# Head 1's K rows shifted by GpSimd instead of copied twice by ScalarE, in a chunk-selected attention with an MLP

## The chip, the core and the metric

The kernel runs on one core of a Trainium2 chip. The core has TensorE (PE, matrix multiplications into PSUM), VectorE (DVE), ScalarE (ACT), GpSimd (POOL), SyncE (SP, here an issuer of DMAs), 16 DMA engines, and the on-chip memories SBUF (128 partitions) and PSUM. GpSimd works on SBUF alone in this kernel. The metric is the device time of one execution, in microseconds.

## The reference

Four batches, eight heads, 768 positions, 64 dimensions a head. For each query, the keys are taken in chunks of 32; an upper bound of the score of each chunk is built from the chunk's elementwise minimum and maximum, the six best chunks that causality allows are kept, and softmax attention runs over these. The result goes through an MLP with 2048 hidden units and an ELU.

```python
k_min, k_max = np.min(k_chunks, axis=3), np.max(k_chunks, axis=3)
ub = np.sum(np.maximum(q * k_min, q * k_max), axis=-1)          # per query and chunk
ub = np.where(causal, ub, -1e9)
top_chunks = np.argsort(ub, axis=-1)[..., -6:]
scores = np.where(sel & causal_by_position, q @ k.T / 8, -1e9)
x = softmax(scores) @ v                                          # 3072 x 512 over all heads
h = x @ w_in
out = np.where(h > 0, h, np.exp(np.minimum(h, 0)) - 1) @ w_out
```

## The kernel before, in words

**Units of work.** Two heads make a pair (16 pairs, four a batch, numbered 0 to 15), two pairs a quad. The 768 positions are worked on in two halves of 384. Batch 0 (pairs 0 to 3, the tuple SPLIT) is prepared half by half in `first_prep`, since it stands at the start; the other batches are prepared pair by pair in `pair_prep`. Selection is `quad_sel`, attention `pair_attend`, the MLP of a batch and half `mlp`.

**Preparing batch 0.** K and Q of a pair and half are loaded row by row (L755), 192 KB each; V follows (L760). The constant EARLY says of how many pairs Q is issued from ScalarE's queue; the rest is issued by SyncE. TensorE turns each tile (L780, six f32 transposes): both heads' 64 dimensions then lie below each other on 128 partitions of PSUM. From the turned K, ScalarE makes two copies into the pair's bf16 tile `lhs` (L797): head 0's 64 partitions to rows 0 to 63 of the first plane, and head 1's partitions 64 to 127 to rows 0 to 63 of the second. VectorE takes the chunks' minima and maxima from the same PSUM (L806) and their difference (L813). From the turned Q, ScalarE makes an f32 copy (L830) and a relu (L837), both for the bounds, and GpSimd casts the copy to bf16 for both heads (L853). GpSimd casts V (L844).

**Selection inside the scores.** Rows 64 to 87 of `lhs` hold a one-hot pattern of the chunks times a large negative number (`econ`, written once per tile by VectorE at L584, from a table that ScalarE makes at L558), and rows 64 to 87 of the query tile `rhs` hold ones where a chunk is not selected. So one matmul over 88 rows gives scores and mask together. For the first 192 positions, where all allowed chunks are selected, these query rows are zero (memsets at L572).

**Selection.** TensorE makes the bounds (L890) from Q, its relu and the chunk tables; VectorE transposes them (L906), takes the eight largest (L918), compares (L923) and transposes back (L929); GpSimd copies the result into `rhs` (L940).

**Attention.** Scores (L995; in the first half of batch 0 TensorE adds the causal mask too, L1001), exp by ScalarE (L1023), the causal mask of diagonal blocks elsewhere by GpSimd (L1042), probabilities times V with a column of ones (L1055), reciprocal and scaling by VectorE (L1068, L1071), and a transpose into `xT`, by TensorE and ScalarE (L1104, L1107) or by VectorE and a DMA.

**MLP.** Up-projection in 16 blocks of 128 hidden units (L1133), exp (L1142), and on some blocks a relu on ScalarE (L1147); VectorE finishes the ELU into `gT` (L1150, or L1183 and L1188); down-projection (L1204), copy (L1213), store (L1218). The weights come in four quarters each, issued by GpSimd (L636, L640).

**Preparing the other batches.** K and Q are loaded in 128-byte pieces (L682), transposed in blocks by VectorE (L694, L712), reduced (L698), cast by GpSimd (L853); the relu for the bounds is ScalarE's (L715, 128x576 f32); V has its own load and cast (L726, L730).

**Order.** Each engine's order is written out as a list of operation numbers (`QUEUE`, lists for DVE, POOL, ACT, SP and PE), found beforehand. `Plan.order` merges the five lists into one program; each engine then executes its own list strictly in order and waits where data or a buffer is not there. Buffers are pools whose sizes stand in `caps`; who gets which buffer follows from that merged order.

Of the kernel before, what the change touches and what calls it, by code (L numbers as in the profile page):

```python
# [12 lines left out]
AF = mybir.ActivationFunctionType  # L13
# [5 lines left out]
S = 768  # L19
# [40 lines left out]
VMERGE = 10  # L60
LAST = ((0, 256), (256, 128), (384, 128))

EARLY = (4, 0)
QUEUE = {
    "DVE": [
# [21 lines left out]
    ],  # L87
    "POOL": [
# [11 lines left out]
    ],  # L100
    "ACT": [
# [20 lines left out]
    ],  # L122
# [8 lines left out]
    ],  # L131
# [295 lines left out]
def kernel(  # L427
# [64 lines left out]
    def place(h, slot):  # L492
# [5 lines left out]
        elif c in kept:  # L498
            tiles[h] = kept[c][slot]
        elif c in shapes:  # L500
            shape, dt = ([P, 8, HALF], F32) if h in STAGED.values() else shapes[c]
            tiles[h] = work.tile(shape, dt, name=f"{c}_{h[1]}", tag=f"{c}{slot}")
# [784 lines left out]
```

## Time and profile before

| | us |
|---|---|
| three runs | 268.28, 263.69, 267.38 |
| their median | 267.38 |
| the profiled execution | 263.55 |
| its span, from the first instruction to the last | 261.8 |
| TensorE busy | 256.1 (98%) |
| VectorE busy | 207.5 (79%) |
| ScalarE busy | 193.1 (74%) |
| GpSimd busy | 121.1 (46%) |

The page of the profile gives busy times of a whole execution. Other views of the same trace cut it into stretches, group instructions by source line, list who waited for whom, or follow the chain of work that ended last. A duration in such a row is that of one instruction unless it says xN; matmuls overlap, so their mean durations add up to more than the time they take. A DMA row gives the time from issue to landing.

### The profile page before, as it was taken

The page shows a single profiled execution, that of the slowest core. Times are in us where ns is not written, and L with a number is a line of the kernel's source. Part 1 is how long each engine was busy: PE and PEld are TensorE (multiplying, and loading weights), DVE is VectorE, ACT ScalarE, POOL GpSimd, SP SyncE. Part 2 cuts the span into 40 slices and gives each one's busy share as a digit, 9 for nine tenths or more (in the row PEclk, how much of TensorE's full clock was granted, in tenths as well). Part 3 has the DMA queues.
Part 4 walks back from the last instruction along what each step waited for, and adds up shares of the span by engine and source line. Part 5 has one row for each costly group of instructions (what it writes and reads, how often), then busy time and mean ns, then how long its engine had stood idle before and what let it go on. Part 6 is the DMA issues. An engine that isn't in the chain of part 4 may idle for free.

```text
span 261.8 us, 6681 instructions
## 1 busy us (share of the span) xinstructions
PE 256.1 (98%) x2416; PEld 158.4 (60%) x2416; DVE 207.5 (79%) x545; ACT 193.1 (74%) x364; POOL 121.1 (46%) x216
## 2 busy tenths in 40 slices
PE   8999989999999999999999999999999999999995
PEld 7888556655556655657555456656565755455544
DVE  4999998999999999998899886987465897335530
ACT  4999989927897899898997567988879554043332
POOL 2688668746737868866641319866302000000000
PEclk9999999999999999999999999999999999999999
DMA  7999999999999979349958393323033012220123
GB/s 218 318 200 170 179 179 133 188 203 134 166 150 213 199 137 134 80 80 210 171 99 179 56 254 82 87 73 95 8 84 106 18 30 66 89 83 12 68 92 112
DMA packets 127010, 33.74 MB, mean 129 GB/s; under 512 B 112897, under 2 KB 124033, under 8 KB 126977
## 3 DMA queue, kind: packets, MB, share of 16 engines
q1 hardware_dynamic: 121664, 28.33, 53.5%
q0 software_dynamic: 4224, 4.19, 10.4%
q10 hardware_dynamic: 1088, 0.79, 1.0%
q8 instruction: 19, 0.31, 0.5%
q14 instruction: 15, 0.11, 0.2%
HBM read 29.23 MB, written 8.26 MB: 143 GB/s over the span
## 4 chain that ended last, share of the span: by engine, by line
PE 83%; DMA 8%; SPq 5%; ACT 1%; ACTq 1%; issue 1%; POOL 0%; POOLq 0%
PE psM L1204 24%; PE psH L1133 22%; PE psS L995 12%; PE psS L1133 8%; PE psO L1055 7%; PE psMT L1204 7%; DMA w_in_sb<-in_moe_w_in_dram 4%; SPq L682 3%; PE psS L890 3%; DMA gT<-in_q_dram 2%; SPq L760 2%; DMA out_dram<-osb 1%; DMA gT<-in_v_dram 1%; ACTq L755 1%; PE psT L1104 1%
## 5 line engine op out<-in xcount | busy, mean ns | idle before, releaser
L1023 ACT ACTIVATE pt<-psS 128x768 bf16<-128x768 f32 (+1 forms) x120 | 89.9, 787 | 10.9 <-PE psS L995 6.2
L1133 PE MATMUL psH<-xT,w_in_sb 128*128 128x384 bf16 x384 | 75.1, 325 | 0.8 <-DMA w_in_sb<-in_moe_w_in_dram 0.8
L1204 PE MATMUL psM<-w_out_sb,gT 128*128 128x512 bf16 x288 | 72.2, 379 | 0.0
L1133 PEld LDWEIGHTS <-w_in_sb 128*128 128x128 bf16 x512 | 47.4, 97 | 33.9 <-issue 1.3
L1204 PEld LDWEIGHTS <-gT 128*128 128x128 bf16 x416 | 37.9, 97 | 34.7 <-issue 0.6
L1142 ACT ACTIVATE f<-psH 128x384 f32<-128x384 f32 x96 | 48.0, 513 | 12.9 <-PE psH L1133 12.4
L995 PE MATMUL psS<-rhs,lhs 88*128 88x384 bf16 (+4 forms) x304 | 53.6, 283 | 0.2
L1042 POOL TENSOR_SCALAR_AFFINE_SELECT pt<-pt 128x256 bf16<-128x256 bf16 (+1 forms) x56 | 28.9, 523 | 47.2 <-ACT pt L1023 46.4
L1055 PEld LDWEIGHTS <-pt 128*128 128x128 bf16 x672 | 31.0, 98 | 10.2 <-ACT pt L1023 0.5
L995 PEld LDWEIGHTS <-lhs 88*128 88x128 bf16 x304 | 26.9, 98 | 13.6 <-ACT pt L1023 1.0
L1055 PE MATMUL psO<-vext,pt 128*128 128x65 bf16 x672 | 34.7, 194 | 0.0
L1150 DVE SCALAR_TENSOR_TENSOR gT<-f,psH 128x384 bf16<-128x384 f32 x48 | 25.5, 541 | 10.7 <-ACT psH L1147 10.6
L853 POOL CAST rhs<-f 64x768 bf16<-64x768 f32 (+1 forms) x40 | 27.6, 692 | 10.7 <-ACT f L830 7.4
L1183 DVE SCALAR_TENSOR_TENSOR t<-f,psH 128x384 bf16<-128x384 f32 x48 | 25.7, 539 | 6.6 <-ACT f L1142 6.3
L940 POOL COPY rhs<-selt 24x576 bf16<-24x576 bf16 (+2 forms) x40 | 22.6, 564 | 18.1 <-DVE selt L929 16.1
L1142 ACT ACTIVATE f<-psS 128x768 f32<-128x768 f32 x16 | 13.0, 814 | 22.9 <-PE psS L1133 22.9
L1188 DVE SCALAR_TENSOR_TENSOR gT<-psH,t 128x384 bf16<-128x384 f32 x48 | 26.1, 549 | 0.8
L1147 ACT ACTIVATE psH<-psH 128x384 f32<-128x384 f32 x48 | 24.6, 520 | 0.0
L1133 PE MATMUL psS<-xT,w_in_sb 128*128 128x384 bf16 x128 | 22.9, 326 | 0.0
L1204 PE MATMUL psMT<-w_out_sb,gT 128*128 128x512 bf16 (+2 forms) x128 | 22.1, 326 | 0.0
L1172 DVE TENSOR_SCALAR t<-f 128x768 bf16<-128x768 f32 x16 | 8.9, 556 | 15.7 <-ACT f L1142 15.7
L853 POOL CAST lhs<-f 64x768 bf16<-64x768 f32 x24 | 19.6, 820 | 0.7
(59 smaller groups left out, 273.4 us busy)
## 6 DMA issues: line engine op xcount, KB each, us to landing
out_dram<-osb SPq DMA_DIRECT2D x23, 256.0 KB, 2.2
f<-in_k_dram SPq DMA_DIRECT2D x48, 96.0 KB, 3.8
f<-in_q_dram SPq DMA_DIRECT2D x48, 96.0 KB, 3.7
f<-in_v_dram SPq DMA_DIRECT2D x10, 384.0 KB, 4.4
w_in_sb<-in_moe_w_in_dram POOLq DMA_DIRECT2D x4, 512.0 KB, 9.1
w_out_sb<-in_moe_w_out_dram POOLq DMA_DIRECT2D x4, 512.0 KB, 7.4
xd<-on SPq DMA_DIRECT2D x80, 24.0 KB, 1.6
xT<-xd SPq DMA_DIRECT2D x20, 96.0 KB, 2.2
```

Of the source, the lines that this page charges most:

```text
L853: nc.gpsimd.tensor_copy(out=o, in_=i)
L995: nc.tensor.matmul(p_s[:, hd, pc:pc + w], lhsT=tiles[pt_["kb"]][0:deep(hd), hd, 128 * kb:128 * kb + 128], rhs=tiles[pt_["qb"]][0:deep(hd), ...
L1023: lambda bs=bs, pt=pt, wtot=wtot, lo=lo, at=at: nc.scalar.activation(out=tiles[pt][:, :, lo:lo + wtot], in_=tiles[bs[0]][:, :, at:at + wto ...
L1042: nc.gpsimd.affine_select(out=a, in_=a, compare_op=AOT.is_ge, fill=0.0, base=0, pattern=pat, channel_multiplier=-1)
L1055: nc.tensor.matmul(po[:, hd, qi, :], lhsT=tiles[pt][:, hd, off:off + 128], rhs=tiles[pt_["vx"]][:, 6 * hd + kb, :], start=(kb == 0), stop= ...
L1133: nc.tensor.matmul(o, lhsT=w_in_sb[:, kk, f0:f0 + 128], rhs=rhs, start=(kk == 0), stop=(kk == NKK - 1))
L1142: lambda e=e, view=view: nc.scalar.activation(out=halves(e)[:, 0:step], in_=view(), func=AF.Exp),
L1147: lambda view=view: nc.scalar.activation(out=view(), in_=view(), func=AF.Relu),
L1150: lambda e=e, view=view, fc=fc, gt=gt: nc.vector.scalar_tensor_tensor(out=tiles[gt][:, fc:fc + step, :], in0=halves(e)[:, 0:step], scalar= ...
L1183: lambda e=e, t=t, view=view: nc.vector.scalar_tensor_tensor(out=tiles[t][:, 0:step], in0=halves(e)[:, 0:step], scalar=1.0, in1=view(), op ...
L1188: lambda t=t, view=view, fc=fc, gt=gt: nc.vector.scalar_tensor_tensor(out=tiles[gt][:, fc:fc + step, :], in0=view(), scalar=0.0, in1=tiles ...
L1204: nc.tensor.matmul(pm, lhsT=tiles[gt][:, fc, 128 * tt:128 * tt + 128], rhs=w_out_sb[:, fc, x0:x1], start=(fc == 0), stop=(fc == NFC - 1))
```

## The change

Names and lines of the diff are those of the kernel before.

- In batch 0, both halves (KSHIFT), ScalarE copies all 128 partitions of the turned K at once into the first plane of `lhs`. Head 1's rows, which now lie on partitions 64 to 127 of that plane, are copied by GpSimd to rows 0 to 63 of the second plane. After that VectorE writes the one-hot rows of the first plane (`mark`), once per pair and half, since the copy has overwritten them. Scores that use the rows wait for the mark, except those of the first 192 positions.
- VectorE no longer writes the first plane's one-hot rows of pairs 0 to 3 at the start.
- The relus of pairs 4 and 5 (RELUP2) are made by GpSimd.
- 14 load buffers `f` instead of 13; four relu buffers `qa` instead of three; a probability tile has 384 columns a head instead of 512.
- In two probability tiles the order of the two key blocks is swapped, so that the two diagonal blocks adjoin.
- Q of pairs 2 and 3 is issued by SyncE (EARLY 2 instead of 4).
- All five lists are new.
- Other new parameters (RELUDVE, RELUPOOL, UBTWO, NXT, NON, NPT) are empty or have the old value.

```diff
+RELUPOOL = ()
+KSHIFT = (0, 1)
+RELUP2 = (4, 5)
+NF = 14
+NQA = 4
...
-EARLY = (4, 0)
+EARLY = (2, 0)
 QUEUE = {
...
-            "f": 13, "qa": 3, "kb": 5, "qb": 5, "vx": 5, "kx": 2, "km": 4,
+            "f": NF, "qa": NQA, "kb": 5, "qb": 5, "vx": 5, "kx": 2, "km": 4,
...
-        "pt": ([P, 2, 512], BF16), "t": ([P, 2, HALF], BF16),
+        "pt": ([P, 2, HALF], BF16), "t": ([P, 2, HALF], BF16),
...
                 r = slice(0, 64) if HIGH and hd else slice(64, 96)
+                if hd == 0 and i < 4 and KSHIFT:
...
+                    continue
                 eng.tensor_copy(out=kept["kb"][i][r, hd, :], in_=econ[r])
...
-        add("ACT", act(S - SEL0) + 0.036, pr + 0.1,
-            lambda: nc.scalar.activation(out=tiles[qa], in_=tiles[qt][:, SEL0:S], func=AF.Relu),
-            reads=[qt], writes=[qa], alloc=[qa])
+        if u in RELUP2:
+            add("POOL", pool(S - SEL0), pr + 0.1,
+                lambda: nc.gpsimd.tensor_scalar_max(tiles[qa], tiles[qt][:, SEL0:S], 0.0),
+                reads=[qt], writes=[qa], alloc=[qa], tag="qrelu2")
...
+    def mark(u, hf, pr):
+        kb = PAIR[u]["kb"]
+        a, b = HALF * hf, HALF * hf + HALF
+        add("DVE", 0.2, pr, lambda: nc.vector.tensor_copy(out=tiles[kb][64:96, 0, a:b], in_=econ[64:96, a:b]),
+            reads=["econ", (kb, hf, 1)], writes=[(kb, hf, "m")], port=True, tag="mark")
...
-        for hd in () if KTWO else range(2):
+        if hf in KSHIFT:
+            add("ACT", act(HALF), pr,
+                lambda: nc.scalar.activation(out=tiles[kb][:, 0, a:b], in_=ps(bk, None, None)[:, :], func=AF.Copy),
+                reads=[bk[0]], writes=[(kb, hf, 0), (kb, hf, "m"), (bk[0], "turn")], alloc=[] if hf else [kb], tag="kcopy0")
+            add("POOL", pool(HALF), pr + 0.02,
+                lambda: nc.gpsimd.tensor_copy(out=tiles[kb][0:64, 1, a:b], in_=tiles[kb][64:128, 0, a:b]),
+                reads=[(kb, hf, 0), (kb, hf, "m")], writes=[(kb, hf, 1)], tag="kcopy1")
+            if hf:
+                mark(u, hf, pr + 0.3)
+        for hd in () if KTWO or hf in KSHIFT else range(2):
...
-        0: [[(0, 0, 384, 0)], [(1, 128, 256, 0), (2, 256, 128, 256)]],
+        0: [[(0, 0, 384, 0)], [(2, 256, 128, 0), (1, 128, 256, 128)]],
...
-            [(3, 384, 384, 0)], [(4, 512, 256, 0), (5, 640, 128, 256)]],
+            [(3, 384, 384, 0)], [(5, 640, 128, 0), (4, 512, 256, 128)]],
...
+                marked = [(pt_["kb"], i, "m") for i in range(hf + 1) if i in KSHIFT] if u in SPLIT else []
+                if marked and hf == 0 and pi == 1:
+                    mark(u, 0, pr - 0.3)
...
-                    + [(pt_["qb"], hf, hd) for hd in range(2)]
+                    + [(pt_["qb"], hf, hd) for hd in range(2)] + marked
...
-                                a = tiles[pt].rearrange("p h (a b) -> p (h a) b", b=256)[:, :, 0:128]
+                                a = tiles[pt][:, :, 0:256]
```

More of the change, by code (lines that the diff above doesn't have):

```diff
@@ L60 @@
 VMERGE = 10
+RELUDVE = ()
+RELUPOOL = ()
+KSHIFT = (0, 1)
+RELUP2 = (4, 5)
+UBTWO = ()
+NF = 14
+NQA = 4
+NXT = 8
+NON = 4
+NPT = 10
 LAST = ((0, 256), (256, 128), (384, 128))
-EARLY = (4, 0)
+EARLY = (2, 0)
 QUEUE = {
     "DVE": [
[21 rows of a table removed]
[22 rows of a table added]
     ],
     "POOL": [
[11 rows of a table removed]
[12 rows of a table added]
     ],
     "ACT": [
[20 rows of a table removed]
[20 rows of a table added]
     ],
     "SP": [
[7 rows of a table removed]
[7 rows of a table added]
     ],
     "PE": [
[32 rows of a table removed]
[31 rows of a table added]
     ],
@@ L438 @@
     caps = {"S2": 2, "ps": 4, "H": 3, "O": 2, "T": 2, "M": 2, "MT": 2,
-            "f": 13, "qa": 3, "kb": 5, "qb": 5, "vx": 5, "kx": 2, "km": 4,
-            "ubt": 1, "thr": 1, "selv": 1, "selt": 2, "pt": 10, "t": 3, "gT": 3,
-            "osb": 3, "on": 4, "rc": 3, "xT": 8}
+            "f": NF, "qa": NQA, "kb": 5, "qb": 5, "vx": 5, "kx": 2, "km": 4,
+            "ubt": 1, "thr": 1, "selv": 1, "selt": 2, "pt": NPT, "t": 3, "gT": 3,
+            "osb": 3, "on": NON, "rc": 3, "xT": NXT}
     plan = Plan(caps)
@@ L499, in place @@
             tiles[h] = kept[c][slot]
+            assert not KSHIFT or c != "kb" or slot < 4 or h not in [PAIR[u]["kb"] for u in SPLIT]
         elif c in shapes:
@@ L583, in f @@
                 r = slice(0, 64) if HIGH and hd else slice(64, 96)
+                if hd == 0 and i < 4 and KSHIFT:
+                    for x in range(2):
+                        if x not in KSHIFT:
+                            eng.tensor_copy(out=kept["kb"][i][r, 0, HALF * x:HALF * x + HALF], in_=econ[r, HALF * x:HALF * x + HALF])
+                    continue
                 eng.tensor_copy(out=kept["kb"][i][r, hd, :], in_=econ[r])
@@ L618 @@
             continue
-        add("DVE", 0.6, (-5.0, -4.0, 0.9, 0.95, 2.0)[i], c_rows(i), reads=["econ"] + (["elow"] if HIGH else []), writes=[("rows", i)], port=True)
+        add("DVE", 0.6 - (0.3, 0.13)[2 - len(KSHIFT)] if i < 4 and KSHIFT else 0.6, (-5.0, -4.0, 0.9, 0.95, 2.0)[i], c_rows(i), reads=["econ"] + (["elow"] if HIGH else []), writes=[("rows", i)], port=True)
     v3 = v.rearrange("b h (n p) d -> p (b h n) d", p=P)
@@ L669 @@
     SELT = {}
+    BU = {}
     XT = {}
@@ L713, in pair_prep @@
             reads=[qd], writes=[qt], alloc=[qt], free=[qd])
-        add("ACT", act(S - SEL0) + 0.036, pr + 0.1,
-            lambda: nc.scalar.activation(out=tiles[qa], in_=tiles[qt][:, SEL0:S], func=AF.Relu),
-            reads=[qt], writes=[qa], alloc=[qa])
+        if u in RELUP2:
+            add("POOL", pool(S - SEL0), pr + 0.1,
+                lambda: nc.gpsimd.tensor_scalar_max(tiles[qa], tiles[qt][:, SEL0:S], 0.0),
+                reads=[qt], writes=[qa], alloc=[qa], tag="qrelu2")
+        else:
+            add("ACT", act(S - SEL0) + 0.036, pr + 0.1,
+                lambda: nc.scalar.activation(out=tiles[qa], in_=tiles[qt][:, SEL0:S], func=AF.Relu),
+                reads=[qt], writes=[qa], alloc=[qa])
         for hd in range(2):
@@ L830, in first_prep @@
             lambda: nc.scalar.activation(out=tiles[qt][:, qo[0]:qo[0] + QW], in_=ps(bq, None, None)[:, 0:QW], func=AF.Copy),
-            reads=[bq[0]], writes=[qt], alloc=[qt], tag="qcopy")
+            reads=[bq[0]], writes=[qt], alloc=[qt], free=bq if (u, hf) in RELUPOOL else [], tag="qcopy")
         lo = max(a, SEL0)
@@ L835, in first_prep @@
         PAIR[u]["ao", hf] = la
-        add("ACT", act(l1 - l0), pr + 0.05,
-            lambda: nc.scalar.activation(out=tiles[qa][:, la:la + l1 - l0], in_=ps(bq, None, None)[:, l0:l1],
-                                         func=AF.Relu),
-            reads=[bq[0]], writes=[qa], alloc=[qa], free=bq, tag="qrelu")
+        if (u, hf) in RELUPOOL:
+            add("POOL", pool(l1 - l0), pr + 0.05,
+                lambda: nc.gpsimd.tensor_scalar_max(tiles[qa][:, la:la + l1 - l0],
+                                                    tiles[qt][:, qo[0] + l0:qo[0] + l1], 0.0),
+                reads=[qt], writes=[qa], alloc=[qa], tag="qrelu")
+        elif (u, hf) in RELUDVE:
+            add("DVE", dve(l1 - l0), pr + 0.05,
+                lambda: nc.vector.tensor_scalar_max(tiles[qa][:, la:la + l1 - l0], ps(bq, None, None)[:, l0:l1], 0.0),
+                reads=[bq[0]], writes=[qa], alloc=[qa], free=bq, tag="qrelu")
+        else:
+            add("ACT", act(l1 - l0), pr + 0.05,
+                lambda: nc.scalar.activation(out=tiles[qa][:, la:la + l1 - l0], in_=ps(bq, None, None)[:, l0:l1],
+                                             func=AF.Relu),
+                reads=[bq[0]], writes=[qa], alloc=[qa], free=bq, tag="qrelu")
         for hd in range(2):
@@ L873, in quad_sel, with ub @@
             bu = new("S2")
-            def ub(bu=bu, c0=c0, n=n, nh=nh):
+            both = whole and g // 2 in UBTWO
+            if both and g % 2:
+                bu = BU[g]
+            def ub(bu=bu, c0=c0, n=n, nh=nh, pairs=pairs):
                 pu = tiles[bu[0]]
@@ L894, in quad_sel @@
             fr = []
-            for u in pairs:
+            for u in pairs if not both else range(4 * (g // 2), 4 * (g // 2) + 4):
                 rd += [PAIR[u]["qt", hf], PAIR[u]["qa", hf]] + [(PAIR[u]["km"], i, x) for i in range(2) for x in hs]
@@ L899, in quad_sel, with ubs @@
                     fr += [PAIR[u]["km"]]
-            add("PE", 0.00167 * n + 0.27, pr, ub, ins=64, reads=rd, writes=[bu[0]], alloc=bu, free=fr)
+            if both and g % 2 == 0:
+                b2 = BU[g + 1] = new("S2")
+                p2 = (pairs[0] + 2, pairs[1] + 2)
+                def ubs(ub=ub, b2=b2, p2=p2):
+                    ub()
+                    ub(bu=b2, pairs=p2)
+                add("PE", 2 * 0.00167 * n + 0.27, pr, ubs, ins=128, reads=rd, writes=[bu[0], b2[0]], alloc=bu + b2, free=fr)
+            elif not both:
+                add("PE", 0.00167 * n + 0.27, pr, ub, ins=64, reads=rd, writes=[bu[0]], alloc=bu, free=fr)
             ut, = new("ubt")
@@ L1027, in pair_attend @@
                         free=bs if si == len(shares) - 1 else [])
-                    done = {0: tiles_by_half[0], 1: tiles_by_half[1]}[hf][ti]
+                    done = ([[(0, 0, 384, 0)], [(1, 128, 256, 0), (2, 256, 128, 256)]] if pieces is FIRST else tiles_by_half[hf])[ti]
                     if pi < len(pieces) - 1 and pieces is FIRST and ti:
@@ L1033, in pair_attend @@
                     diag = [pc for (kb, c0, w, pc) in done if c0 == 128 * kb]
+                    assert onpe or diag in ([], [0], [0, 128])
                     if diag and not onpe:
@@ L1138, in mlp @@
                     free=[XT[4 * b + kk] for kk in range(NKK)] if hf and fc == NFC - step else [])
-                both = fc in BOTH[b]
+                both = fc in BOTH.get((b, hf), BOTH[b])
                 e, = new("f")
```

183 rows, old and new, of the table QUEUE are left out of this document.

## The prediction

> **What bounds the kernel now.** I read the busy shares first, then TensorE's busy time in stretches, then the waits and the chain of the stretch that is not full.
>
> ```profile
> PE 256.1 (98%) x2416; PEld 158.4 (60%) x2416; DVE 207.5 (79%) x545; ACT 193.1 (74%) x364; POOL 121.1 (46%) x216
> 0.00:4.00 4.00, 2.94 (x28) 2.90 (x28) 1.44 (x8) 1.11 (x1) 1.85 (x16) 1.00 0.47 140
> 4.00:24.00 20.00, 19.85 (x292) 17.44 (x289) 18.21 (x77) 18.87 (x47) 12.96 (x28) 1.00 1.08 243
> 24.00:40.00 16.00, 14.41 (x165) 8.91 (x164) 14.89 (x42) 15.26 (x30) 11.20 (x23) 1.00 1.13 181
> 40.00:100.00 60.00, 60.00 (x605) 36.01 (x604) 58.75 (x139) 49.95 (x92) 41.43 (x66) 1.00 1.07 170
> 100.00:160.00 60.00, 60.00 (x536) 34.97 (x535) 54.11 (x154) 48.56 (x95) 31.69 (x50) 1.00 0.71 141
> ```
>
> The columns after the length are TensorE, its weight loads, VectorE (DVE), ScalarE (ACT), GpSimd (POOL), then the granted clock and the DMA share. From 40 us on TensorE is full (60.00 of 60.00), and the number of its instructions is the same in both kernels. So time can be won only where TensorE is idle: 0.15 us between 4 and 24, 1.59 between 24 and 40, 1.74 in all, beside the start. The ends of matmuls are modelled, so each gap may hide a little more; I allow as much again, 3.6 us, as the most that this change can give. In the same two stretches ACT (18.87 of 20, 15.26 of 16) and DVE (18.21, 14.89) are nearly full and POOL is not (12.96, 11.20). The change takes work from ACT and gives it to POOL and DVE in just these stretches.
>
> What TensorE waits for between 4 and 40 us, and the chain up to the longest of these waits:
>
> ```profile
> PEld L1104 <- DVE on L1071: 1.3, 3, 0.6
> PEld L995 <- ACT pt L1023: 1.0, 3, 0.5
> PE psH L1133 <- DMA w_in_sb<-in_moe_w_in_dram: 0.8, 1, 0.8
> PEld psS L890 <- ACT lhs L797: 0.2, 1, 0.2
> ...
> 2.37 5.91 DMA gT<-in_q_dram
> 25.71 0.64 POOL w_in_sb L636
> 26.35 10.04 DMA w_in_sb<-in_moe_w_in_dram
> 36.44 0.84 PE psH L1133 x4
> ```
>
> The longest single gap (0.8) is the third quarter of w_in: issued by POOL at 26.35, landed at 36.39, needed by the sixth up-projection in TensorE's list (fc 8). Waits on ACT come to 1.2 (scores waiting for an exp to free their PSUM, and one for a K copy); waits on DVE's normalized outputs stand ahead of the transposes that feed the first MLP.
>
> **The change part by part.** Rows for the prices:
>
> ```profile
> L797 ACT ACTIVATE lhs<-psH 64x384 bf16<-64x384 f32 x16 | 7.8, 485 | 0.8 <-PE psH L780 0.7
> L830 ACT ACTIVATE f<-psMT 128x384 f32<-128x384 f32 x8 | 3.9, 493 | 0.2 <-PE psMT L780 0.2
> L715 ACT ACTIVATE qa<-f 128x576 f32<-128x576 f32 x12 | 8.3, 692 | 0.8 <-DVE f L712 0.8
> L844 POOL CAST vext<-gT 128x384 bf16<-128x384 f32 x8 | 3.9, 503 | 0.4
> L730 POOL CAST vext<-f 128x768 bf16<-128x768 f32 x12 | 9.9, 824 | 4.0 <-DMA f<-in_v_dram 3.7
> 16.89 0.34 POOL L940 COPY rhs<-selt 24x192 bf16<-24x192 bf16 x1
> 10.01 0.62 DVE L584 COPY lhs<-econ 32x768 bf16<-32x768 bf16 x2
> 8.16 0.76 DVE L584 COPY lhs<-econ 32x768 bf16<-32x768 bf16 x2
> ```
>
> *K copies.* Of 16 ACT copies of 0.485, eight remain (all 128 rows at once; 64 rows took 0.485 and 128 rows of the same 384 columns 0.493, so I keep 0.485). ACT loses 8 x 0.485 = 3.9 us, all before 25 us. POOL gets eight shifts of 64x384 bf16: at least 0.34 (a 24x192 copy), at most 0.50 (a 128x384 cast); I take 0.50, the same length, so +4.0 us on an engine that has 11.8 idle in 4 to 40. The chain for one head is no longer: the second ACT copy, 0.485 behind the first, becomes a shift of 0.50 behind it. In POOL's new list five shifts stand among the first casts and three (second half, pairs 1 to 3) behind the second quarter of w_in.
>
> *Marks.* The shift leaves head 1's rows where the one-hot chunk rows belong, so DVE writes these back afterwards: eight copies of 32x384. Before, the same rows were written once by 32x768 copies, 0.31 each where nothing disturbs them; four of these go (1.24). A mark is between half of that (0.155) and all of it (0.31); I take 0.2, so 1.6 against 1.24, net +0.4. Behind each mark in DVE's list stand the reductions, the chunk selection and the normalizations, so this lands on the waits for L1071 above. Against it stands an earlier start:
>
> ```profile
> 0.80 2.06 ACTq L755 DMA_DIRECT2D gT<-in_q_dram  x4
> gT<-in_k_dram SPq DMA_DIRECT2D x1, 192.0 KB, 3.2
> 0.81 3.89 SPq L755 DMA_DIRECT2D gT<-in_k_dram  x5
> 2.89 1.28 ACT L558 ACT_TABLE_LOAD   x1 [2.89 <-issue]
> 1.38 1.05 DVE L572 MEMSET rhs<- 32x192 uint32 x5
> 5.06 1.16 DVE L584 COPY lhs<-econ 32x768 bf16<-32x768 bf16 x4 [2.63 <-ACT econ L558]
> 4.11 1.09 PEld L780 LDWEIGHTS psH<-ident_f,gT 128*128 128x128 f32 x6
> 6.51 0.67 PEld L780 LDWEIGHTS psH<-ident_f,gT 128*128 128x128 f32 x6
> ```
>
> *Two Q loads leave ACT's queue.* Two issues of some 0.5 fewer: the table load moves from 2.89 to about 1.9 and DVE's first copies, which wait 2.63 for the table's product, by as much. I set this 1.0 against the net 0.4 and the memsets that now stand behind those copies (1.05 in the list, formerly before them), and cost DVE at nothing; bounds 0.5 less to 3.2 more (eight marks of 0.56, that is 0.31 and a blocked quarter, less 1.24).
>
> On SP these two loads, and second-half K loads, now stand ahead of the K of pairs 1 to 3; TensorE's second group of transposes is pair 0's Q, the second load of ACT's queue, where it was the first. The first load lands at 4.0 (0.81 + 3.2), the eighth at 8.28 (2.37 + 5.91), 0.6 apart, so this one is there near 5.9, while the first transposes end near 5.2 to 5.4. A gap of 0.6, of which later slack takes half: +0.3. Bounds 0 and 1.9, for a rest there may also keep the transposes slow: the first six took 1.09, the same six 0.67 from 6.51 on, with the granted clock at 1.00 in both; three groups at that rate are 1.3 more. The Trainium skill (TensorE: Matmul & The Clock Gate, Part 1) has the array at half rate until a window of some 3.4 us was busy, and the slow and fast group agree with it.
>
> ```profile
> 41.40 0.65 PE psH L1133 x4
> 28.37 0.50 POOL L940 COPY rhs<-selt 24x384 bf16<-24x384 bf16 x1
> 30.10 0.40 POOL L1042 TENSOR_SCALAR_AFFINE_SELECT pt<-pt 128x256 bf16<-128x256 bf16 x1 [0.66 <-ACT pt L1023]
> ```
>
> *Weights.* The third quarter's consumer moves from the sixth to the eighth up-projection, two groups of 0.65 and some scores later, so at least 1.3 later than now; the wait of 0.8 goes, if the quarter does not land more than 1.3 later. In POOL's list it now stands behind two shifts, two V casts, two selection copies and a mask.
>
> *Relus.* ACT loses 2 x 0.692 near 45 to 49 us, where TensorE is full: no gain. POOL pays between 0.65 (three quarters of the 128x768 cast) and 0.824 each, 1.4 in all. If POOL were late there, batch 1's first bounds would wait; priced at the whole 1.4, kept for the range.
>
> *Rest.* Masks over adjoining columns have the same counts and sizes; a probability tile of 384 columns, a 14th load buffer and a 4th relu buffer add no instruction. What they release sooner are loads, and TensorE is not waiting for loads after 40 us: 0.
>
> *Sum*, on the profiled execution's own 263.55 (span 261.8): the weight wait -0.8, of the 1.2 of waits on ACT 1.0 since ACT gets 3.9 back, the gap at the start +0.3: **262.0**. The three runs shown have a median of 267.38, two of them 3.8 and 4.7 above the profiled one. No view says what these two spent; the changed kernel may well have such runs too, so the range reaches there.
>
> **The rivals.**
>
> *Hidden anyway, 263.5.* DVE, not ACT, paces the stage before the first MLP: 1.3 us of waits on L1071 against 1.0 on ACT's exps, and DVE gains no room. Then each wait on ACT that goes is taken up by one on DVE and the weight wait shifts to the next quarter. For it: DVE's 14.89 of 16. Against it: the weight wait is on the chain, not on DVE.
>
> *Slower: the third quarter of w_in is late, 265.8.* The seven POOL instructions ahead of it cost 6 x 0.5 and a mask of 0.4, so it is issued near 29.8 to 30 instead of 26.35. If it takes 10.0 from there as now, it lands near 40, at least 3 us after its new place in TensorE's list (36.44 - 0.8 + 1.3); 263.55 - 0.8 + 3 is 265.8. It decides from a landing after 37. Against it: 10.0 was spent behind the second quarter, issued just ahead; the first took 6.2.
>
> ```profile
> DMA to landing us min/median/max: 6.2/9.1/11.6
> 17.28 0.50 POOL L853 CAST rhs<-f 64x384 bf16<-64x384 f32 x1
> 17.40 0.54 DVE L923 TENSOR_TENSOR selv<-ubt,thr 128x144 bf16<-128x144 f32 x1
> 14.00 0.29 DVE L923 TENSOR_TENSOR selv<-ubt,thr 128x144 bf16<-128x144 f32 x1
> ```
>
> *Slower: POOL and DVE block each other, 267.* The same DVE instruction took 0.29 where POOL rested and 0.54 under a POOL cast; the copies at 8.16 took 0.76 for two, against 0.62. The change puts 4.0 us more POOL work and eight more such copies into one stage. If each mark costs 0.56, DVE's list is 3.2 longer, and 263.55 + 3.2 + 0.3 is 267. It decides where marks take over 0.4. The Trainium skill (SBUF — State Buffer, Who interferes with whom) says that a GpSimd instruction and a DVE copy of this sort, or one with two SBUF inputs, hold a shared pair of ports exclusively, the later one waiting whole; the row of 0.54 agrees. If every mark waited out one shift of 0.50, that rule alone gives 4.0 us on DVE and 267.6.
>
> *All waits gone, 260.5.* The new order removes the DVE waits too (1.3): 262.0 - 1.3 - 0.2.
>
> **How the numbers follow.** Forecast 0.46, hidden anyway 0.20, weights late 0.13, ports 0.11, all gone 0.10. The range runs from 259.8, just under the most that idle TensorE can give (263.55 - 3.6), to 268.0, which holds both slower cases and the level of the slower two runs. 2% is about what a measurement of this kernel tells from no change; against the median of 267.38 it lies at 262.0 and 272.7. Half of the forecast's share lies under 262.0, and all of the case of 260.5, some of the hidden one: 0.36 faster. Slower by 2% takes one of the slower cases with a run of the upper level, or two causes at once: 0.12. The rest, 0.52, is within.
>
> **What would show it.** Right: TensorE's idle time between 24 and 40 us under 0.8, no up-projection waiting for w_in, eight ACT K copies near 0.485, shifts near 0.50, marks near 0.2, TensorE full from 40 us on. Wrong: marks over 0.4; w_in's third quarter landing after 37 with TensorE waiting; an idle stretch of TensorE after 40 us, above all at batch 1's bounds behind POOL's relus; or transposes still at 1.09 for six after 7 us.

## The result: slower by 0.9%, and the profile after

| | us |
|---|---|
| before, 20 runs | median 266.50 (263.69 to 271.72) |
| changed kernel, 20 runs | median 267.71 (266.90 to 268.70) |
| ratio after to before | 1.0087, 95% interval 1.0067 to 1.0106 |
| profiled execution after, its span | 268.29, 266.6 |

The ratio is of fast runs alone: six of before's 20 runs, from 267.83 up, are left out as slow, which puts its median at 265.40, while over all 20 the two medians lie 0.5% apart. The forecast was 262.0. The time lies in the range that was given and within 2%, but on the other side: some 2.3 us lost (265.40 to 267.71) instead of 1.5 won on the profiled execution. Part of the distance to 263.55 is that execution itself: a second profile of the kernel before took 265.0, a second one of the changed kernel 267.11. The profiled execution of before stands at the low end of that kernel's runs.

The page's busy times after, and TensorE's stretches (length; TensorE, weight loads, DVE, ACT, POOL; granted clock, DMA share, GB/s):

```profile
PE 256.8 (96%) x2416; PEld 158.6 (60%) x2416; DVE 209.9 (79%) x549; ACT 191.0 (72%) x354; POOL 128.4 (48%) x226
4.00:24.00 20.00, 17.82 (x257) 15.40 (x256) 18.55 (x75) 13.20 (x34) 12.96 (x28) 1.00 1.00 237
24.00:40.00 16.00, 13.85 (x184) 9.51 (x183) 15.78 (x50) 14.54 (x28) 13.83 (x27) 1.00 1.18 175
40.00:100.00 60.00, 59.53 (x574) 35.99 (x572) 58.41 (x141) 48.06 (x88) 44.59 (x70) 1.00 1.11 164
100.00:160.00 60.00, 58.95 (x560) 34.48 (x559) 54.00 (x151) 51.01 (x99) 34.44 (x54) 1.00 0.70 143
```

The first two stretches in the second profile of the kernel before:

```profile
4.00:24.00 20.00, 18.59 (x281) 15.82 (x280) 18.54 (x74) 18.37 (x46) 12.61 (x27) 1.00 1.06 239
24.00:40.00 16.00, 15.06 (x177) 9.49 (x174) 15.70 (x44) 16.00 (x31) 11.86 (x24) 1.00 1.16 186
```

TensorE's idle time from 4 to 40 us was 1.74 in the first profile of before and is 2.35 in the second (20 - 18.59 and 16 - 15.06); after it is 4.33, and 4.05 in the second profile of the changed kernel. So 1.7 of the 2.1 us between the two second profiles lie in this stretch. TensorE is not quite full behind it either: from 40 to 160 us it idles 1.52 after the change (60 - 59.53 and 60 - 58.95), 0.51 in the second profile of before, 0 in the first. ACT was relieved as meant: 18.87 and 18.37 busy in the first of these stretches, now 13.20. DVE was not: 18.55, and 15.78 of 16 in the second.

What TensorE waits for between 4 and 40 us after the change (total, times, longest), and what ACT waits for:

```profile
PE psT L1169 <- DVE on L1136: 1.0, 2, 0.6
PE psS L1056 <- POOL rhs L1001: 0.9, 1, 0.9
PE psO L1120 <- ACT pt L1087: 0.7, 1, 0.7
PE psH L809 <- DMA gT<-in_k_dram: 0.4, 1, 0.4
...
PE psMT L809 <- DMA gT<-in_q_dram: 0.3, 1, 0.3
```

```profile
ACT lhs L822 <- PE psH L809: 2.7, 5, 1.4
ACT pt L1087 <- PE psS L1062: 2.5, 4, 1.1
ACT f L868 <- PE psMT L809: 2.0, 4, 1.0
```

The new instructions as groups (busy us, mean ns):

```profile
L822 ACT ACTIVATE lhs<-psH 128x384 bf16<-128x384 f32 x8 | 4.0, 495 | 2.7 <-PE psH L809 2.7
L825 POOL COPY lhs<-lhs 64x384 bf16<-64x384 bf16 x8 | 4.2, 526 | 3.6 <-ACT lhs L822 3.2
L734 POOL TENSOR_SCALAR qa<-f 128x576 f32<-128x576 f32 x2 | 3.3, 1648 | 0.1
```

The marks' line by itself (shortest, median and longest in ns, first and last start):

```profile
L759 DVE COPY lhs<-econ x8: 239/330/536, 10.9 to 39.6; 32x384 bf16<-32x384 bf16 x8
```

No up-projection of this stage waits for w_in any more, but ACT now waits for TensorE's transposes and scores, and TensorE waits for normalized outputs (DVE), for what POOL writes into the query tile (`rhs`) behind DVE's selection, and for an exp. Four steps on the way to the first MLP (the first and the third selection, the last normalization, the first exp of the MLP), before and then after:

```profile
14.33 0.38 DVE L929 STREAM_TRANSPOSE selt<-selv 128x192 bf16<-128x192 bf16 x1
22.92 0.58 DVE L929 STREAM_TRANSPOSE selt<-selv 128x384 bf16<-128x384 bf16 x1
27.28 1.02 DVE L1071 TENSOR_TENSOR on<-psO,rc 128x384 bf16<-128x384 f32 x2
30.58 0.54 ACT L1142 ACTIVATE f<-psH 128x384 f32<-128x384 f32 x1
```

```profile
17.45 0.37 DVE L990 STREAM_TRANSPOSE selt<-selv 128x192 bf16<-128x192 bf16 x1
26.72 0.53 DVE L990 STREAM_TRANSPOSE selt<-selv 128x384 bf16<-128x384 bf16 x1
30.39 0.54 DVE L1136 TENSOR_TENSOR on<-psO,rc 128x384 bf16<-128x384 f32 x1
33.24 0.92 ACT L1207 ACTIVATE f<-psH 128x384 f32<-128x384 f32 x2
```

The first selection comes 3.1 us later, the third 3.8, the last normalization ahead of the first MLP ends 2.6 later and the MLP's first exp starts 2.7 later. Some 0.8 to 1.0 of each is what two executions of the kernel before differ by: in its second profile the two selections start at 15.37 and 23.82 and the exp at 31.37.

### The profile page after: what moved, and what is told of

Its sections match the earlier page's. It is cut to its first block, busy times and chain, and to the rows that moved or that the text cites. A ratio compares the mean times of both kernels' runs of the same rounds, so it can differ in the third digit from the quotient of the medians.

```text
span 266.6 us, 6687 instructions
## 1 busy us (share of the span) xinstructions
PE 256.8 (96%) x2416; PEld 158.6 (60%) x2416; DVE 209.9 (79%) x549; ACT 191.0 (72%) x354; POOL 128.4 (48%) x226
## 4 chain that ended last, share of the span: by engine, by line
PE 77%; DMA 6%; SPq 4%; POOL 4%; ACT 4%; issue 2%; DVE 1%; ACTq 0%; POOLq 0%
PE psM L1269 22%; PE psH L1198 20%; PE psS L1056 10%; PE psMT L1269 8%; PE psS L1198 8%; PE psO L1120 6%; ACT pt L1087 3%; SPq L700 2%; PE psS L942 2%; SPq L789 2%; DMA gT<-in_k_dram 2%; DMA xT<-xd 2%; DMA gT<-in_q_dram 2%; POOL qa L734 1%; DMA f<-in_q_dram 1%
## 5 line engine op out<-in xcount | busy, mean ns | idle before, releaser
L1087 ACT ACTIVATE pt<-psS 128x768 bf16<-128x768 f32 (+2 forms) x120 | 90.6, 785 | 13.8 <-PE psS L1056 8.9
L1198 PEld LDWEIGHTS <-w_in_sb 128*128 128x128 bf16 x512 | 48.0, 97 | 34.3 <-issue 3.1
L1207 ACT ACTIVATE f<-psH 128x384 f32<-128x384 f32 x96 | 47.2, 506 | 12.2 <-PE psH L1198 10.4
L1056 PEld LDWEIGHTS <-lhs 88*128 88x128 bf16 x304 | 25.3, 97 | 14.4 <-issue 1.0
```

Source lines behind the costliest of these rows:

```text
L1056: nc.tensor.matmul(p_s[:, hd, pc:pc + w], lhsT=tiles[pt_["kb"]][0:deep(hd), hd, 128 * kb:128 * kb + 128], rhs=tiles[pt_["qb"]][0:deep(hd), ...
L1087: lambda bs=bs, pt=pt, wtot=wtot, lo=lo, at=at: nc.scalar.activation(out=tiles[pt][:, :, lo:lo + wtot], in_=tiles[bs[0]][:, :, at:at + wto ...
L1198: nc.tensor.matmul(o, lhsT=w_in_sb[:, kk, f0:f0 + 128], rhs=rhs, start=(kk == 0), stop=(kk == NKK - 1))
L1207: lambda e=e, view=view: nc.scalar.activation(out=halves(e)[:, 0:step], in_=view(), func=AF.Exp),
```

## The experiments

All ratios are against runs of the kernel before on the same chip in the same session, with 6 to 12 runs of each version; intervals are 95%. "New" lists go with all else that is new in the changed kernel (loads, buffers, the order of the key blocks); the old lists with a shift (e6, e7, e11, e12, e17) run with its probability tiles and key blocks.

| run | lists | shift | ratio, interval |
|---|---|---|---|
| e4_before_again | old | none | 1.0036, 0.9996 to 1.0075 |
| e5_lists_alone | new | none | 1.0086, 1.0058 to 1.0114 |
| e6_shift_old_lists | old | 8 | 1.0139, 1.0089 to 1.0189 |
| e7_half_shift_old_lists | old | 4 | 1.0030, 0.9998 to 1.0062 |
| e8_after_again | new | 8 | 1.0111, 1.0065 to 1.0156 |
| e1_relu_act | new | 8, ACT's relus | 1.0110, 1.0073 to 1.0146 |
| e2_no_shift | new | none, POOL's relus | 1.0072, 1.0043 to 1.0102 |
| e3_no_marks | new | 8, no marks | 1.0056, 1.0021 to 1.0090 |
| e11_marks_by_act | old | 8, marks by ACT | 1.0046, 1.0016 to 1.0077 |
| e12_no_marks_old_lists | old | 8, no marks | 1.0030, 1.0002 to 1.0058 |
| e13_first_halves_first | new, other loads | 8 | 1.0104, 1.0056 to 1.0153 |
| e14_after_marks_by_act | new | 8, marks by ACT | 1.0201, 1.0157 to 1.0244 |
| e15_both | as e13 | 8, marks by ACT | 1.0185, 1.0138 to 1.0232 |
| e9_table_earlier | old | none | 1.0013, 0.9974 to 1.0052 |
| e10_table_and_row_later | old | none | 0.9979, 0.9948 to 1.0009 |
| e16_rows_before_reductions | old | none | 1.0034, 1.0004 to 1.0064 |
| e17_half_shift_mended | as e16 | 4 | 1.0054, 1.0028 to 1.0081 |

The first row is the yardstick: the kernel before against itself gave 1.0036, so nothing within about 0.4% of 1 is read as a difference here.

**First session: the parts of the change, one at a time.** The theory was that ACT does not bound this stage, so its relief gains nothing, while DVE's marks and blocked copies and the new order cost; the rivals were POOL's relus, and chance.

```
e1  -RELUP2 = (4, 5)  +RELUP2 = ()      relus in ACT's list again
e2  -KSHIFT = (0, 1)  +KSHIFT = ()      second K copy behind the first in ACT's list
e3  mark: -nc.vector.tensor_copy(...)  +nothing   (selection of head 0 in batch 0 then not applied)
e4  the kernel before
```

> The changed kernel with the relus of pairs 4 and 5 back on ScalarE, put into ScalarE's list behind the exps of up-projection blocks 14 and 15; everything else as changed. If POOL's 1.65 us a relu (0.69 on ScalarE) is what TensorE waits for between 40 and 56 us, the kernel comes out 1 to 2 us under the changed one's 267.7, at 265.7 to 266.7, with TensorE's hidden gaps between 40 and 56 us (about 1.3 us before the bounds of quad 2) gone. If the loss lies before 40 us (marks, locks, load order), at most 0.5 under, 267.2 to 267.7.

> The changed kernel with batch 0's K copied twice by ScalarE again (no shifts on POOL, no marks on DVE, the one-hot rows written once at the start); all lists otherwise as changed. If the marks and the port between POOL and DVE make DVE's list longer in the stage before the first MLP, DVE gets back about 2.8 (marks) + 1.1 (key-range differences) - 1.4 (rows) = 2.5 us and the kernel comes out 1.5 to 2.5 under the changed one, 265.2 to 266.2, with the last selection transpose of quad 0's first half back from 17.45 to about 15.5. If ScalarE's relief is worth what was forecast (1.0) and DVE is not the pace, it comes out slower than the changed one, 268.5 to 269. If the order of loads and lists sets the stage, within 0.5 of the changed one.

> The changed kernel without the eight mark instructions: the one-hot rows of batch 0's first plane are left out, so its selection for head 0 of batch 0 is not applied; shifts and lists stay. If DVE paces the stage, the 2.8 us of marks come back as 1.5 to 2.8 us, 264.9 to 266.2. If the order of loads and lists, or the relus, set it, 267.2 to 267.7.

> The kernel before once more, unchanged: a second profile of it, since its 20 runs spread from 263.7 to 271.7 and the first profile (263.55) lies at the low end. Expected 264 to 268, ratio 1.000 within 0.005. If the first profile is typical of its order, TensorE is idle 0.1 to 0.3 us between 4 and 24 us again, and the spread lies elsewhere (a late transfer in the middle). If its first stage is the part that varies, the idle time of TensorE before 40 us differs from 1.74 by as much as the time differs from 263.55.

POOL's relus are not the cause: with them back on ACT the time stayed (1.0110). Without the shift and without the marks the kernel stayed slower than before, 1.0072 and 1.0056. So a part of the loss is neither relu nor mark. The kernel before, run again, showed 0.61 us more idle time of TensorE before 40 us in an execution 1.45 longer: its first stage varies, but that is not the whole of what varies.

**Second session: order against shift.** The lists without the shift, the shift without the lists, half of it, and the whole.

```
e5  -KSHIFT = (0, 1)  +KSHIFT = ();  -RELUP2 = (4, 5)  +RELUP2 = ()
e6  before's lists and loads;  +KSHIFT = (0, 1), shift in POOL's list, marks in DVE's
e7  as e6;  KSHIFT = (0,)
e8  the changed kernel
```

> The changed kernel's lists, load order and buffers, but without the shift, without the marks and with ACT's relus: each half of batch 0's K is copied twice by ACT, as in the kernel before. Theory one (the new lists hold up the stage before the first MLP, above all because second-half K loads and reductions now stand ahead of the first chunk selection): still slower than before by 0.5 to 0.9 per cent (ratio 1.005 to 1.009), TensorE's idle time before 40 us 3.4 to 4.2 us, the first transpose of a selection by DVE after 16.5 us. Theory two (shift and marks hold it up, by DVE's and POOL's shared port): ratio 0.998 to 1.003, idle time before 40 us about 2.

> The kernel before in its own lists and load order, with the shift for all eight copies: ACT copies 128 rows once, POOL shifts, DVE marks; the marks of the first half stand in DVE's list behind the scores that they must follow, the others right behind the second reduction of the same half. Theory one (lists): within 0.3 per cent of before, ratio 0.997 to 1.003, the first selection's transpose within 1 us of the 14.33 of before. Theory two (shift and marks): slower by 0.4 to 1.2 per cent (1 to 3 us), TensorE's idle time before 40 us over 3, marks over 0.4 on average. A gain of over 0.3 per cent would mean that ACT's relief does count when the order of before is kept.

> As the run before, but only the first halves of the four pairs are shifted (four shifts, four marks); the second halves are copied twice by ACT. Theory one: ratio 0.997 to 1.003, as in the run before. Theory two: half of what the run before loses, 0.2 to 0.6 per cent.

> The changed kernel once more, unchanged, beside the others on the same chip: ratio 1.006 to 1.011 by both theories, TensorE's idle time before 40 us between 3.8 and 4.8, so that the other runs can be set against it.

Each theory was borne out in its own run and neither sufficed, and the marks in e6 took less than theory two had asked for (0.37 on average, not over 0.4). The new lists alone cost 0.9% (2.2 us), the shift alone, in the old order, 1.4% (3.7 us), and together they cost 1.1%: they do not add up. On the new lists the shift adds 0.25%, which the intervals do not tell from nothing; the lists themselves are slower than the old ones. Half a shift cannot be told from none.

The lists alone already show most of what the changed kernel shows. TensorE idles 3.88 us from 4 to 40 us (18.16 of 20 and 13.96 of 16 busy), and its three longest waits are those of the changed kernel, with the same sizes:

```profile
PE psT L1161 <- DVE on L1128: 1.0, 2, 0.6
PE psS L1048 <- POOL rhs L993: 0.9, 1, 0.9
PE psO L1112 <- ACT pt L1079: 0.7, 1, 0.7
```

What DVE waits for there, and two steps of its list:

```profile
DVE km L836 <- ACT lhs L827: 1.5, 4, 0.6
25.27 0.97 DVE L704 STREAM_TRANSPOSE f<-f 128x768 f32<-128x768 f32 x1
26.17 0.53 DVE L982 STREAM_TRANSPOSE selt<-selv 128x384 bf16<-128x384 bf16 x1
```

The third selection starts at 26.17, 3.25 us later than in the first profile of before and 2.35 later than in the second, without any shift or mark. In the new order a normalization (0.55) and a block transpose of batch 1 (0.97) stand ahead of it, which in before stand behind it, and DVE's reductions wait 1.5 us for ACT's K copies, where in before they do not wait. So the place is known; that the later selection is what the 0.9% pays for is not shown.

The old order shows where the shift costs. DVE's groups up to 28 us (busy us, mean ns), in the two profiles of before:

```profile
L584 DVE COPY lhs<-econ 32x768 bf16<-32x768 bf16 x10 | 3.2, 361 | 2.7 <-ACT econ L558 2.6
L813 DVE TENSOR_TENSOR km<-kx,km 128x12 f32<-128x12 f32 x8 | 1.4, 191 | 0.0
L923 DVE TENSOR_TENSOR selv<-ubt,thr 128x144 bf16<-128x144 f32 (+1 forms) x3 | 1.3, 429 | 0.0
```

```profile
L584 DVE COPY lhs<-econ 32x768 bf16<-32x768 bf16 x10 | 4.1, 451 | 2.7 <-ACT econ L558 2.6
L813 DVE TENSOR_TENSOR km<-kx,km 128x12 f32<-128x12 f32 x8 | 2.0, 271 | 0.0
```

In e6_shift_old_lists, and what TensorE waits for there between 4 and 40 us:

```profile
L750 DVE COPY lhs<-econ 32x384 bf16<-32x384 bf16 x8 | 2.9, 374 | 0.2
L592 DVE COPY lhs<-econ 32x768 bf16<-32x768 bf16 x6 | 2.5, 436 | 2.7 <-ACT econ L561 2.6
L842 DVE TENSOR_TENSOR km<-kx,km 128x12 f32<-128x12 f32 x8 | 2.2, 294 | 0.0
L975 DVE TENSOR_TENSOR selv<-ubt,thr 128x144 bf16<-128x144 f32 (+1 forms) x3 | 1.6, 545 | 0.0
```

```profile
PE psT L1160 <- DVE on L1127: 1.4, 2, 1.2
PE psS L1047 <- DVE ubt L958: 1.2, 1, 1.2
...
```

Its third selection and its first normalization (start, length):

```profile
27.65 0.56 DVE L981 STREAM_TRANSPOSE selt<-selv 128x384 bf16<-128x384 bf16 x1
28.33 1.02 DVE L1127 TENSOR_TENSOR on<-psO,rc 128x384 bf16<-128x384 f32 x2
```

Against the first profile of before, DVE's list is longer by 2.9 (marks) - 0.7 (rows: six copies at 436 ns instead of ten at 361) + 0.8 (differences) + 0.3 (comparisons) = 3.3 us. The third selection comes 4.7 us later (22.92 to 27.65), and the kernel takes 3.7 more. Against the second profile of before (rows 4.1, differences 2.0) the list is longer by 1.8 only, the selection 3.8 later; so the likeness of 3.3 to 3.7 is partly the choice of the profile.

**Third session: marks off DVE, and DVE relieved.** If DVE's work is what costs, moving the marks to ACT must give most of it back, and taking work from DVE in the kernel before must win.

```
e9   -EARLY = (4, 0)  +EARLY = (2, 0), the two loads in SP's list; the rest as before
e10  as e9; DVE: rows of the fifth buffer moved from batch 0's reductions to the first MLP
e11  as e6; mark: -nc.vector.tensor_copy(...)  +nc.scalar.activation(..., func=AF.Copy)
e12  as e6; no marks
```

> The kernel before, but the Q loads of pairs 2 and 3 are issued by SP instead of ACT, so that ACT's table load and the econ rows come about 1 us earlier and DVE's first copies with them; every other list is that of before, and the order of the loads too. Theory one (DVE paces the stage before the first MLP, so every microsecond taken from it there shortens the kernel): DVE's first normalization 0.5 to 1.0 us earlier than in before, 0.3 to 1.0 us won, ratio 0.996 to 0.999. Rival (the stage is paced by the landing of the loads, not by DVE): ratio 0.999 to 1.002, DVE's gain turns into idle time of DVE before its reductions.

> The run before, and DVE writes the one-hot rows of the fifth K buffer (0.6 us, needed only by batch 1) behind the first operations of the first MLP instead of between batch 0's reductions. Theory one: another 0.3 to 0.6 us, ratio 0.993 to 0.998. Rival: no difference from the run before, within 0.2 per cent.

> The lists of before with the shift, as in the run e6_shift_old_lists, but the eight marks are written by ACT instead of DVE, so DVE has 1.24 us less to do than in before and 2.9 less than with the marks, and ACT about as much as 8 times 0.35 to 0.5 more. Theory one (DVE's own added work is what the shift costs): 2 to 3 us of the 3.7 of that run come back, ratio 0.997 to 1.005. Rival (POOL's shifts block DVE through the shared port, or the scores wait for the longer chain of copy, shift and mark): less than 1 us comes back, ratio 1.009 to 1.014.

> The lists of before with the shift, without any mark (leaves out the one-hot chunk rows of head 0's plane of batch 0, so the selection there is not applied rightly). Theory one: DVE is 1.24 us lighter than in before, ratio 0.995 to 1.003. Rival (port or chain): ratio 1.006 to 1.012.

The first half was borne out: with the marks on ACT 0.9 of the 1.4% came back (1.0016 to 1.0077 against 1.0089 to 1.0189), and leaving them out gave no more that can be measured. That is the marks' price in the old lists, and it is DVE's, since the same eight copies cost ACT 4.0 us there and the kernel stands where before stood against itself:

```profile
L751 ACT ACTIVATE lhs<-econ 32x384 bf16<-32x384 bf16 x8 | 4.0, 517 | 0.2
```

The second half was not: with the table 1 us earlier, and with two row copies less in the stage, no gain can be measured.

**Fourth session: what is wrong with the new lists.** The suspects were the loads of second halves put ahead of the first selection, and the marks on DVE there too.

```
e13  SP: first halves' K and Q first; pair 0's second half (PE, ACT, POOL, DVE) behind the first bounds
e14  the changed kernel, marks by ACT
e15  both
```

> The changed kernel, but the loads of all first halves of K and Q come before those of the second halves, in the order in which TensorE uses them, and the transposes, the copy, the shift, the reductions and the mark of pair 0's second half move behind the first bounds in the lists of their engines; nothing else moves. Theory (the new lists cost time because pair 0's second half was put ahead of the first selection, which then comes 2 to 3 us later than in before): DVE's first selection transpose (17.45 in the changed kernel, 14.33 in before) at 15.0 to 16.3, a third to all of the 0.9 per cent back, ratio 1.002 to 1.007. Rival (the order does not matter, DVE's amount of work does): ratio 1.008 to 1.011 as in the changed kernel, DVE's first normalization again near 25.

> The changed kernel with the eight marks written by ACT instead of DVE, nothing else. Theory (DVE's added work costs time, ACT's does not, since ACT waits in this stage): about what leaving the marks out gave (1 us), ratio 1.003 to 1.007. Rival (ACT's marks delay exps and copies as much as DVE's delayed selections): ratio 1.008 to 1.012.

> Both edits of the two runs before: first halves first, marks by ACT. If both causes are right and add up: ratio 0.997 to 1.003, that is, no slower than before, with ACT's K copies halved. If it stays over 1.005, a third cause (POOL's shifts in a full list, or the order of the scores and exps) is behind the rest.

The theory missed in all three; e13 came out as its rival had it. With first halves first, the first selection came at 16.36 (17.45 in the changed kernel), just past what was aimed at, the third at 25.64 (26.72), and the start gap went. But TensorE's idle time from 4 to 40 us stayed (4.34); its waits came back elsewhere:

```profile
PE psS L1047 <- POOL rhs L992: 1.2, 1, 1.2
PE psMT L800 <- DVE kx L835: 1.0, 1, 1.0
```

With the marks on ACT, the new lists lost another 1%, where the old ones had won. In the new order ACT's marks stand among its exps, and TensorE waits for these: longest at 20.89 us, 1.3 for an exp right behind a mark, and 1.0 in the first MLP's stage. The stretch from 24 to 40 us also ran at a lower granted clock:

```profile
24.00:40.00 16.00, 13.66 (x173) 9.73 (x172) 13.48 (x40) 13.64 (x27) 12.02 (x22) 0.90 1.11 165
```

```profile
PE psS L1048 <- ACT pt L1079: 2.5, 3, 1.3
```

How much of that 1% is the order and how much the clock is not settled: one run of e14 at a granted clock of 0.999 took 270.02, hardly less than the five at 0.992 to 0.994 (270.16 to 271.67), while one run of e15 at 1.000 took 268.19 against 270.07 to 271.55. In the profiles of both, the clock falls to 0.50 for 2 us (24 to 26 in e14, 22 to 24 in e15), each time 2 us after a stretch of 2 us in which TensorE was busy for only 0.83 and 0.82 us. In e6 TensorE was busy 0.87 us from 22 to 24 and the clock stayed at 1.00, so such a stretch alone does not explain it. So the reason for the new lists' own 0.9% stays open: it is not the order of the loads alone, not the relus, and not the shift.

**Fifth session: DVE undisturbed.** A last attempt to turn the explanation into a gain: all of pair 0 to 3's row copies written before POOL's first cast.

```
e16  as e10; DVE: pair 1's rows moved ahead of pair 0's reductions
e17  as e16; KSHIFT = (0,)
```

> The kernel before without any shift, with the three things that take DVE's row copies out of POOL's way: SP issues the Q loads of pairs 2 and 3, so the table comes 1 us earlier; the rows of the fifth buffer are written behind the first operations of the first MLP; and pair 1's rows, which stand between pair 0's and pair 1's reductions (0.76 and 1.04 for two copies there under POOL casts, 0.62 elsewhere), are written ahead of all reductions, before POOL's first cast. Theory (DVE's work and its blocking by POOL pace the stage before the first MLP): 0.5 to 1.3 us faster than before, ratio 0.995 to 0.998. Rival (DVE's early gain is lost in waits for TensorE's transposes): 0.998 to 1.002.

> The run before with the shift of the first halves only (four shifts, four marks on DVE, as in e7_half_shift_old_lists). Theory: it pays for the marks what that run paid, 0.2 to 0.5 per cent over the run before, ratio 0.998 to 1.003. Rival (with DVE relieved, ACT's relief counts at last): under the run before, ratio below 0.995.

In e16 the copies took 346 ns, and DVE's first normalization came 0.44 us earlier than in the first profile of before (23.25 against 23.69). TensorE's waits there:

```profile
PE psH L1126 <- DVE gT L1181: 0.7, 1, 0.7
PE psT L1097 <- DVE on L1064: 0.5, 2, 0.2
PE psH L1126 <- DMA w_in_sb<-in_moe_w_in_dram: 0.3, 1, 0.3
```

The first MLP waited for a quarter of w_in and for DVE's own ELU, so the gain seems to have turned into new waits. The half shift in this order came out at 1.0054: ACT's relief does not count there either. No version here beats the kernel before by more than can be measured.

## Why the prediction was wrong, point by point

**What had no term at all was the largest:** that all five lists are new. The prediction followed the order where the diff moved a step (loads, weights, marks) and gave the rest of it no term. The lists without the shift lose 2.2 us (1.0086), most of the some 3 that the changed kernel lost in the same session (1.0111), and the one thing in them that the prediction did look at, second-half loads ahead of first-half ones, is not by itself what costs (e13). What in the lists does cost stays open. The range held the time only because it had been opened for the slower cases.

**The view was right, its weight was not.** In the first profile TensorE was full after 40 us, and the change could win only the idle 1.74 before; that is also why the most it could win was small. What the sum did not hold is that several engines bind this stage almost at once (TensorE, ACT and DVE were all over 90% busy from 4 to 24 us). Relief of ACT without the marks won nothing (e12), relief of DVE alone won nothing (e16), and work added to DVE cost time (e6).

**"Of the 1.2 of waits on ACT 1.0" (-1.0) failed.** Those 1.2 were waits of weight loads, which run beside the matmuls. The matmuls themselves waited for w_in (0.8) and for this:

```profile
PE psT L1104 <- DVE on L1071: 0.5, 2, 0.2
```

Of the idle 1.74 that leaves some 0.4 for ACT at most, so 1.0 was more than was there. And the scores' waits on exps did go down, but the products with V now wait 0.7 for one, and ACT's 3.9 us turned into ACT's own waits (2.7, 2.5 and 2.0 above). The rival "hidden anyway" had this mechanism and named DVE as what paces; its price, 263.5, was too low since it let DVE's own work stay the same.

**"DVE at nothing" failed.** The marks took 0.33 at the median, 0.36 on average and up to 0.54, where 0.2 was taken. The rows' saving arrived in the changed kernel (six copies at 348 ns) and only 0.7 of it in the old lists (six at 436). The differences, with two inputs, took 294 ns, against 191 in the first profile of before and 271 in the second. The upper bound of 3.2 is what the old order showed against the first profile (3.3; 1.8 against the second). The earlier start that was set against it is worth nothing measurable (e9). The Trainium skill (SBUF — State Buffer, Who interferes with whom) says that a DVE copy in a mode that uses both port pairs, or a DVE instruction with two SBUF inputs, and a GpSimd instruction that reads SBUF shut each other out for whole instructions. The rows agree: the same ten copies of the same program took 361 ns on average in one execution and 451 in another, and in the second a pair that ran under two POOL casts (8.21 to 9.29) took 1.04, where in the first a pair took 0.62 while POOL rested (at 6.47):

```profile
8.46 1.04 DVE L584 COPY lhs<-econ 32x768 bf16<-32x768 bf16 x2
```

That rule had been priced as a rival, 267, deciding from marks over 0.4. Its time is near the measured 267.71, but by luck: the marks stayed under 0.4, and the lists without shift and marks lose most of it (e5).

**The weights (-0.8): the wait went, the gain did not come.** Prediction and rival both asked when the third quarter lands. It was issued 6.6 us later than before (32.97 against 26.35) and took at most 7.4:

```profile
32.97 0.76 POOL L653 DMA_DIRECT2D w_in_sb<-in_moe_w_in_dram  x1
```

```profile
DMA to landing us min/median/max: 5.7/7.1/7.4
```

It therefore landed after 38.6, later than the 37 at which the rival was to decide, and nobody waited, because the MLP itself started 2.7 later. A wait that goes because its consumer has become later is no gain.

**The start gap (+0.3): named rightly, counted at half.** TensorE waited 0.4 for a K load and 0.3 for a Q load; 0.6 was named and half of it counted. But the gap is not the change's alone: in its second profile the kernel before waits 0.9 for a K load too. Its first two groups of six transposes took 0.85 and 0.82 us there, and 1.51 and 1.35 in the first profile, which therefore counts as busy what is idle time in the second; 1.74 was a low figure to start from. **The shifts: right**, 0.50 at the median. **ACT's copies: right**, 0.495.

**The relus: size wrong by two, conclusion right.** 1.65 each against at most 0.824 (and the lower bound, three quarters of that, is 0.62 and not 0.65), and moving them back changed nothing.

## What to carry to other kernels

Where two or three engines are over 90% busy in the same stage, price the added work of a change at its worst bound and its relief at nothing, until a view shows one engine that everything waits for. Count as TensorE's idle time what its matmuls wait for, not what its weight loads wait for beside them. When all orders are new, that is a part of the change with a price of its own, to be tried by itself. And run the old kernel against itself before believing a few tenths of a per cent.

## What the runs showed of the hardware that was not expected

- POOL's f32 maximum with a constant over 128x576 took 1.648 us, 2.9 ns a column, while its cast of 128x768 took 0.824, 1.1 ns a column. The Trainium skill (GPSIMD Engine Reference, 4.1 Engine selection) has one-input elementwise work there at roughly line rate; the row differs, and the row decides.
- ACT's copy of 32 partitions took as long as one of 128: 517 ns for 32x384, 495 for 128x384.
- The kernel before spread over 8 us in 20 runs, the changed one over 1.8. Two profiles of the kernel before differ by 1.5 us in DVE's row copies and differences before 28 us (3.2 and 1.4 against 4.1 and 2.0), which goes with 263.55 against 265.0. The times near 269 look different: in the profiles of e9 (269.11) and e17 (269.56) a Q load of batch 1 took 7.3 and 7.2 us, DVE waited 3.6 and 1.8 for it, and TensorE 3.4 and 1.7 behind DVE. That these two are the whole of the spread was not tested.
